# One written order for all engines over the attention, the first weights and the first nine steps

## The chip, the core and the metric

The kernel runs on one core of one Trainium2 chip. The metric is device time in microseconds (us), from three runs before the change. Engines are called by the profile's names: PE (TensorE, matmul), PEld (its weight load), DVE (VectorE), ACT (ScalarE), POOL (GpSimd) and SP (SyncE, which issues all DMAs here).

## The reference, cut to what matters

Attention between x (4 batches, 8 heads, 512 tokens, 64 wide) and a state of 32 rows per head, in both directions; then two dense feed-forward layers over the 2176 rows of 512 that come out. Weights come as float64, x and state as float32.

```python
a = softmax(scale * x @ state.T);  xread = a @ state         # 512 rows per batch and head
a2 = softmax(scale * state @ x.T); sread = a2 @ x            # 32 rows per batch and head
x = concat(xread, sread) -> (4 * 544, 512)
h = x @ moe_w_in                                             # 512 x 2048
x = (maximum(h, 0) + log1p(exp(-abs(h)))) @ moe_w_out        # softplus, 2048 x 512
g = x @ w_gate; val = x @ w_val                              # 512 x 1536 each
out = (g * sigmoid(g) * val) @ w_out2                        # 1536 x 512
```

## The kernel before, in words

**Precision.** Matrices are float32 split in two parts of a shorter format, a high part (a copy on ACT) and a low part (whole less high, on POOL or DVE, line 77); a product is three matmuls (`mm3`, line 74). A weight arrives as int64 raw words (`Piece`, line 101): 128 rows x 512 values, 512 KB. `head` is two DVE instructions on the upper words (lines 117, 121), `square` is ACT (line 127), `tail` is two on DVE (line 131 for the lower words, line 135, which multiplies by a comparison with TINY so that values too small become zero). Then `high` (ACT, line 141) and `low` (POOL). w_in is used whole (t of the piece), w_out split.

**Attention.** There are eight items (b, par), each four heads of one batch: 128 rows (4 heads x 32 state rows) by 512 tokens. Scores on PE (line 259), row maximum on DVE (264), its negation (266), exponent with row sum on ACT (269), transposition of the scores in blocks of 32 on DVE (273), maximum over groups of 32 (280), subtraction on POOL (283), exponent on ACT (288), sums (292 to 295) on DVE, product on POOL (298), transposition back on DVE (304), high and low part (308, 77) into aT. Besides, PE transposes the first exponent (322), ACT copies it (324), PE multiplies it with x (334), ACT scales it (338), and after two items PE turns the result (342, "psr") and ACT copies it into sw (343).

**First layer.** The first product, of attention weights by state by w_in, is taken as (state @ w_in) first: m, in `m_mm` (line 353), with high on ACT (357) and low on DVE. w_in and w_out are cut in four chunks of 512 columns. A unit is (chunk c, batch b, ft), 64 in all. `p1` is six matmuls (three per par) into a "ph" bank; ACT reads it twice for the softplus (high 383, whole 386), POOL makes the low part l (`g_low`, 77); `p2` is twelve matmuls into four banks "py" that collect over the four ft of a batch. After ft 3 `y_add` takes the four banks to yacc: DVE copies for chunk 0 (line 428), DVE additions after that (line 430). In step n, PE runs p2 of unit n and p1 of unit n + 4 (LAG). The rows of the state go through s1 to s4 once per chunk (s1: line 482).

**Order.** Hooks `at(n, kind, fn)` hang pieces of other work on the steps: in a step the kinds run as load, pe, softplus, dve0, y_add, act, g_low, pool, y_add, dve1, act1, pool1. `tc.manual_schedule(engines=...)` binds an engine to the order in which the program issues. For the attention that is PE alone, for the main loop PE, DVE and SP; ACT and POOL are ordered by the framework's scheduler by its own estimate. The attention is issued by `place(when, fn)` with times that sort it; all weights of the first chunk go through `whole` there, in the gaps.

**Loads.** All go by SP in order: the state, x transposed in halves of 64 partitions of 256 KB (`load_xt`, line 95: item par 0 the lower half of two tiles, par 1 the upper), x in rows (`load_xn`, 99) 512 KB per item, pieces. xT has four buffers, so that x of the last batches waits for the first scores.

**Second layer.** Lines 797 to 898; its weights are made in the background during the first layer (`second_piece`, EARLY: 18 of 36 pieces) and in its own steps. Per column block PE forms seven products px, pz, py ("quad"), ACT copies them (854, 866, 873), DVE adds (862, 877, 881, 886). Sums of y for it (T, lines 446 to 452, and their low parts) are made on DVE and POOL in the last steps of the first layer.

Of the kernel before, what the change touches and what calls it, by code (L numbers as in the profile page):

```python
# [16 lines left out]
P = 128  # L17

TINY = 1.125 * 2.0 ** -30
# [3 lines left out]
def attention_moe_moe2_kernel(  # L23
# [37 lines left out]
    SLOTS = {"aT": 8, "mt": 8,  "wo": 6, "yacc": 8, "s": 2, "xT": 4, "T": 14, "made": 3, "w2": 4, "gw": 8}  # L61
# [28 lines left out]
    def load_xt(b, par):  # L90
        q = slice(par * D, (par + 1) * D)
        for h in range(2):
            if par == 0:
                xT[b, h] = slot([P, 2, S], F32, "xT", f"xT{b}_{h}")
            nc.sync.dma_start(out=xT[b, h][q], in_=xt_d[b, h, q])
# [4 lines left out]

    class Piece:


        def __init__(self, views, tag, name):
            self.tag, self.name = tag, name
            self.raw = rawp.tile([P, 512], I64, tag="raw", name=f"raw_{name}")
# [5 lines left out]

        def head(self):

            self.t = rawp.tile([P, 512], F32, tag=f"t{self.tag}", bufs=6 if self.tag == "win" else 2, name=f"t_{self.name}")
# [12 lines left out]

        def tail(self):
            ti = self.t.bitcast(I32)  # L130
            nc.vector.scalar_tensor_tensor(
                out=ti, in0=self.bot, scalar=29, in1=ti, op0=ALU.logical_shift_right, op1=ALU.bitwise_or,
            )
# [12 lines left out]
        def whole(self):  # L146
            for step in (self.head, self.square, self.tail):
                step()
            if self.tag != "win":
                self.high()  # L150
                self.low()

# [783 lines left out]
```

## Time and profile before

| | |
|---|---|
| runs | 791.03, 794.01, 796.45 us; median 794.01 |
| profiled execution | 790.25 us, its span 788.5 us |
| mean granted clock of PE | 0.984 |
| busy PE, PEld, DVE | 742.0, 576.4, 493.9 us |
| busy ACT, POOL | 320.3, 397.2 us |
| DMA | 143.79 MB, mean 182 GB/s |

The span is from the first to the last instruction of the profiled execution. Busy times of matmuls are modelled at their ends, and matmuls overlap. A row with "idle before us <-" gives the time that the engine waited just before such instructions, and what ended the wait.

### The profile page before, as it was taken

The page shows a single profiled execution, that of the slowest core. Times are in us where ns is not written, and L with a number is a line of the kernel's source. Part 1 is how long each engine was busy: PE and PEld are TensorE (multiplying, and loading weights), DVE is VectorE, ACT ScalarE, POOL GpSimd, SP SyncE. Part 2 cuts the span into 40 slices and gives each one's busy share as a digit, 9 for nine tenths or more (in the row PEclk, how much of TensorE's full clock was granted, in tenths as well). Part 3 has the DMA queues.
Part 4 walks back from the last instruction along what each step waited for, and adds up shares of the span by engine and source line. Part 5 has one row for each costly group of instructions (what it writes and reads, how often), then busy time and mean ns, then how long its engine had stood idle before and what let it go on. Part 6 is the DMA issues. An engine that isn't in the chain of part 4 may idle for free.

```text
span 788.5 us, 10190 instructions
## 1 busy us (share of the span) xinstructions
PE 742.0 (94%) x3640; PEld 576.4 (73%) x3640; DVE 493.9 (63%) x697; ACT 320.3 (41%) x576; POOL 397.2 (50%) x352
## 2 busy tenths in 40 slices
PE   7476989999999999998789999999999999999997
PEld 2234756777777777786677888888888888888885
DVE  4899447766878668789657857675563343333343
ACT  3456433543444445454354444433253223323320
POOL 2367426444655555789468667665355113212311
PEclk9997998999999999999899999999999999999999
DMA  9942114343334333454939798978437646535502
GB/s 228 323 131 80 54 45 146 118 120 130 135 109 132 136 126 115 138 202 141 338 112 356 280 368 324 319 267 329 160 120 284 219 138 218 191 125 208 185 35 107
DMA packets 51202, 143.79 MB, mean 182 GB/s; under 512 B 5840, under 2 KB 18128, under 8 KB 51152
## 3 DMA queue, kind: packets, MB, share of 16 engines
q1 hardware_dynamic: 51152, 143.15, 53.6%
q8 instruction: 28, 0.46, 0.2%
q14 instruction: 22, 0.18, 0.1%
HBM read 107.22 MB, written 35.91 MB: 182 GB/s over the span
## 4 chain that ended last, share of the span: by engine, by line
PE 48%; DMA 1%; DVE 1%; ACT 1%; POOL 1%; issue 0%; ACTq 0%; DVEq 0%
PE po L74 16%; PE px L74 16%; PE pz L74 8%; PE py L74 6%; PE pt L74 3%; DMA gw<-gv_d 1%; DVE t_gv L121 0%; DMA gv_d<-gv 0%; POOL l L77 0%; DVE T L450 0%; PE pts L600 0%; POOL gv L77 0%; ACT h L551 0%; ACT cC L873 0%; DVE cA L881 0%
## 5 line engine op out<-in xcount | busy, mean ns | idle before, releaser
L74 PE MATMUL py<-h,wo 128*128 128x512 f32 x512 | 160.9, 396 | 10.7 <-DVE yacc L430 6.3
L77 POOL TENSOR_TENSOR l<-C,h 128x512 fp32r<-128x512 f32 x64 | 93.3, 1460 | 72.2 <-PE py L74 52.5
L74 PE MATMUL po<-w,h 128*128 128x512 f32 x384 | 126.3, 391 | 0.0
L74 PEld LDWEIGHTS py<-h,wo 128*128 128x128 f32 x512 | 97.1, 191 | 32.4 <-DVE yacc L430 7.1
L77 POOL TENSOR_TENSOR l<-cA,h 128x512 fp32r<-128x512 f32 x24 | 35.5, 1481 | 146.0 <-ACT h L551 146.0
L74 PE MATMUL ph<-aT,m 128*128 128x512 f32 x384 | 102.9, 406 | 0.0
L74 PE MATMUL py<-l,wo 128*128 128x512 f32 x256 | 101.1, 395 | 0.9 <-POOL l L77 0.9
L74 PEld LDWEIGHTS ph<-aT,m 128*128 128x128 f32 x384 | 72.5, 193 | 28.3 <-issue 11.5
L572 DVE TENSOR_TENSOR oacc<-po,oacc 128x512 f32<-128x512 f32 x80 | 54.7, 690 | 56.4 <-PE po L74 56.0
L74 PEld LDWEIGHTS po<-w,h 128*128 128x128 f32 x384 | 72.1, 188 | 14.8
L74 PE MATMUL po<-w,l 128*128 128x512 f32 x192 | 74.9, 390 | 0.5 <-POOL l L77 0.5
L74 PE MATMUL px<-T_0s,gw 128*128 128x512 f32 x216 | 61.0, 391 | 3.3 <-ACT cC L873 3.3
L74 PE MATMUL px<-T_1s,gw 128*128 128x512 f32 x216 | 60.7, 390 | 0.0
L74 PEld LDWEIGHTS py<-l,wo 128*128 128x128 f32 x256 | 48.8, 191 | 11.8 <-POOL l L77 1.4
L383 ACT ACTIVATE h<-ph 128x512 fp32r<-128x512 f32 x64 | 38.0, 593 | 33.8 <-PE ph L74 33.7
L74 PEld LDWEIGHTS px<-T_0s,gw 128*128 128x128 f32 x216 | 40.1, 188 | 12.7 <-ACT cC L873 4.1
L862 DVE TENSOR_TENSOR cA<-py,cA 128x512 f32<-128x512 f32 x24 | 16.5, 689 | 49.7 <-PE py L74 47.4
L74 PEld LDWEIGHTS px<-T_1s,gw 128*128 128x128 f32 x216 | 40.6, 188 | 8.5
L189 POOL TENSOR_TENSOR sums_gv<-t_gv 128x128 f32<-128x128 f32 x48 | 25.1, 541 | 40.4 <-DVE t_gv L135 40.4
L551 ACT ACTIVATE h<-cA 128x512 fp32r<-128x512 f32 x24 | 15.2, 632 | 71.7 <-DVE cA L881 70.4
L430 DVE TENSOR_TENSOR yacc<-py,yacc 128x512 f32<-128x512 f32 x48 | 31.7, 687 | 17.3 <-PE py L74 17.3
L74 PEld LDWEIGHTS po<-w,l 128*128 128x128 f32 x192 | 36.1, 188 | 8.3 <-POOL l L77 1.0
(150 smaller groups left out, 1410.1 us busy)
## 6 DMA issues: line engine op xcount, KB each, us to landing
gw<-gv_d SPq DMA_DIRECT2D x96, 512.0 KB, 6.6
gv_d<-gv SPq DMA_DIRECT2D x24, 512.0 KB, 3.3
gv_d<-split_gv SPq DMA_DIRECT2D x24, 512.0 KB, 3.4
w<-w_d SPq DMA_DIRECT2D x24, 512.0 KB, 9.3
raw_win<-in_moe_w_in_dram SPq DMA_DIRECT2D x16, 512.0 KB, 4.4
raw_wo<-in_moe_w_out_dram SPq DMA_DIRECT2D x16, 512.0 KB, 3.9
raw_gv<-in_moe_w_gate_dram SPq DMA_DIRECT2D x48, 128.0 KB, 3.0
raw_gv<-in_moe_w_val_dram SPq DMA_DIRECT2D x48, 128.0 KB, 2.8
```

The source lines that it names most:

```text
L74: nc.tensor.matmul(o, a[s], b[t], start=first and i == 0, stop=last and i == 2, **k)
L77: eng.tensor_tensor(out=o, in0=whole, in1=high.bitcast(F32), op=ALU.subtract)
L189: nc.gpsimd.tensor_tensor(out=o, in0=x, in1=y, op=op)
L383: nc.scalar.activation(self.h, self.ps, AF.Softplus)
L430: nc.vector.tensor_tensor(out=v, in0=yps[dt], in1=v, op=ALU.add)
L551: nc.scalar.activation(h, src, AF.Copy)
L572: nc.vector.tensor_tensor(out=v, in0=ps, in1=v, op=ALU.add)
L862: nc.vector.tensor_tensor(out=c["A"], in0=y, in1=c["A"], op=ALU.add)
```

## The change

1. `Piece`: `head` and `square` become `size` (ACT: the upper words as floats times 2^-112 into t, so that small values become zero there) and a `head` of one DVE instruction on t; `tail` has two DVE instructions (sign bit from the upper words, bits of the lower words). The multiplication of line 135 is gone. In DVE instructions a piece costs three instead of four; ACT's step now comes first instead of second.
2. `load_xt` loads a whole 128-partition tile (512 KB); an item needs both tiles of its batch. xT has eight buffers, raw words of the first chunk six of their own, later pieces two, and the other tiles of the attention have their own buffers (t 8, a2 6, e 4, t2 3).
3. All 25 first loads are issued in one list, LOADS, ahead of all else. The rest up to step 8 is one written list, ORDER: items' steps (`STEPS`), pieces of w_in and w_out of chunk 0 ("i", "o") and of w_in of chunk 1 ("j"), m ("mm", "mh", "ml"), p1 ("p"), softplus ("sp"), g_low ("gl"), p2 ("P"), y_add ("y" with a to d). Items 6 and 7 stand ahead of 5 and 4. The sums' additions and reciprocals (`parts`, `parts_1`) are made once for both items of a batch. All engines but the DMA queues follow it: PE, DVE, SP, ACT and POOL are bound to the order issued, in the main loop too.
4. The main loop starts at step 9 (FIRST). s1 to s4 of chunk 0 come at steps 9 to 15 (before 7 to 13), m of chunk 1 at 9, 12, 15, 19 (before 8, 11, 15, 19), w_out of chunk 1 at 9, 10, 12, 13, the three early second-layer pieces of chunk 0 at 11, 14, 15.
5. `y_add` of chunk 0 copies two of the four banks on ACT. Second-layer steps keep their places, with `size` and `head` where `head` and `square` were.

```diff
-TINY = 1.125 * 2.0 ** -30
+LOADS = "st x01 w0 x00 x11 x10 w1 w2 x31 x20 x30 x21 w3 n11 o0 o1 n10 n00 n01 n21 o3 n30 n31 n20 o2"
+ORDER = (
+    "iab0 ihd0 itl0 sc0 sc1 ts0 mx0 ts1 sc2 M0 M1 mi0 nm0 mx1 iab1 mx2 mi1 ex0 ts2 e0 ihd1 iab2 sc3 S0 ex1",
+    "itl1 pa0 a0 ihd2 S1 nm2 M2 e2 r0 mi2 pa2 mx3 nm1 ts3 a2 ti0 nm3 e1 M3 ti1 e3 tu0 sc6 rc0 ex2 rc2 pa3 mi3",
+    "tu1 iab3 pa1 ts6 ah1 sc7 ihd3 ex3 oab0 M6 al1 sc5 a3 mx7 a1 ts7 pr3 mi6 ah0 ts5 oab1 al0 M7 pr2 ex6 M5",
+    "sr3 mx5 mi7 sr2 nm7 mx6 pr0 e7 mi5 nm5 S3 e5 st1 nm6 pa7 S2 e6 pr1 itl3 sr0 so1 pa6 ex5 r2 itl2 sc4 sr1",
+    "a6 a7 st0 S6 ti3 mm1 oab3 ts4 so0 ex7 pa5 mx4 ti2 mh1 pr6 tu3 a5 ml1 pr7 ah3 nm4 tu2 e4 al3 M4 mm0 ah2",
+    "S5 mi4 pr5 S7 mh0 rc4 oab2 ml0 al2 pa4 sr5 r6 ex4 p0 rc6 a4 S4 ti7 sr7 r4 sr6 mm2 sp0 ohd0 pr4 ohd1 otl0",
+    "p1 mh2 gl0 tu7 sr4 st3 owh0 p2 ml2 ah7 otl1 so3 sp1 st2 p3 owl0 owh1 mm3 so2 owl1 sp2 P0 gl1 mh3 sp3 ml3",
+    "gl2 mm4 jab0 gl3 p4 mh4 ohd2 ml4 ti4 P1 sp4 otl2 gl4 tu4 owh2 mm6 ah4 owl2 jab1 p5 mh6 ohd3 P2 sp5 jhd0",
+    "otl3 gl5 ml6 owh3 mm7 owl3 p6 mh7 jtl0 P3 sp6 al7 ml7 jab2 gl6 mm5 ti5 ya3 yd3 yb3 yc3 p7 mh5 ti6 tu5",
+    "ml5 ah5 P4 al4 tu6 sp7 al5 ah6 al6 p8 gl7 P5 sp8 jhd2 gl8 jtl2 p9 jhd1 P6 sp9 jtl1 gl9 jab3 jhd3 p10",
+    "jtl3 P7 sp10 gl10 p11 ya7 yb7 yc7 yd7 P8 sp11 gl11 p12",
+)
+FIRST = 9
...
+        def size(self):
+            self.t = rawp.tile([P, 512], F32, tag=f"t{self.tag}", bufs=6 if self.tag == "win" else 3, name=f"t_{self.name}")
+            nc.scalar.activation(self.t, self.top.bitcast(F32), AF.Copy, scale=2.0 ** -112)
+
         def head(self):
             ti = self.t.bitcast(I32)
             nc.vector.tensor_scalar(
-                out=ti, in0=self.top, scalar1=3, scalar2=0x3FFFFFF8,
-                op0=ALU.logical_shift_left, op1=ALU.bitwise_and,
+                out=ti, in0=ti, scalar1=3, scalar2=0x7FFFFFF8, op0=ALU.logical_shift_left, op1=ALU.bitwise_and,
             )
+
+        def tail(self):
             nc.vector.scalar_tensor_tensor(
-                out=ti, in0=self.top, scalar=-0x40000000, in1=ti, op0=ALU.bitwise_and, op1=ALU.bitwise_or,
+                out=ti, in0=self.top, scalar=-0x80000000, in1=ti, op0=ALU.bitwise_and, op1=ALU.bitwise_or,
             )
-        def square(self):
-            self.mag = self.top.bitcast(F32)
-            nc.scalar.activation(self.mag, self.mag, AF.Square)
...
             nc.vector.scalar_tensor_tensor(
                 out=ti, in0=self.bot, scalar=29, in1=ti, op0=ALU.logical_shift_right, op1=ALU.bitwise_or,
             )
-            nc.vector.scalar_tensor_tensor(
-                out=self.t, in0=self.mag, scalar=TINY, in1=self.t, op0=ALU.is_gt, op1=ALU.mult,
-            )
...
+        if c == 0 and dt % 2:
+            nc.scalar.activation(v, yps[dt], AF.Copy)
+        elif c == 0:
             nc.vector.tensor_copy(v, yps[dt])
...
-    M_STEPS = (8, 11, 15, 19)
+    M_STEPS = (9, 12, 15, 19)
...
-        with tc.manual_schedule(engines={ENG.DVE, ENG.SP}):
-            for n in range(1 - LAG, NU):
+        with tc.manual_schedule(engines={ENG.DVE, ENG.SP, ENG.Activation, ENG.Pool}):
+            for key in LOADS.split():
+                first_load(key)
+            for names in ORDER:
+                do(names)
+            room[0] = "m"
+            for n in range(FIRST, NU):
```

## Rows read from the trace of the kernel before

**Rows 1.** The page's busy table, PE's entry (us, share, instructions).
```profile
PE 742.0 (94%) x3640; PEld 576.4 (73%) x3640; DVE 493.9 (63%) x697; ACT 320.3 (41%) x576; POOL 397.2 (50%) x352
```

**Rows 2.** Windows by stage: us, busy time of each engine, clock, DMA share, GB/s.
```profile
0.00:73.18 73.18, 46.91 (x413) 21.52 (x413) 57.72 (x118) 35.59 (x73) 33.81 (x33) 0.93 0.68 197
...
114.50:125.50 11.00, 7.08 (x31) 3.95 (x31) 9.53 (x13) 3.87 (x7) 6.23 (x7) 0.69 0.68 231
125.50:340.00 214.50, 214.50 (x1046) 162.85 (x1045) 158.66 (x205) 102.12 (x187) 121.52 (x110) 1.00 0.38 125
```

**Rows 3.** PE's waits from 74 us on: for whom; us in total, times, longest.
```profile
PE py L74 <- DVE yacc L430: 6.3, 2, 5.0
PE py L74 <- DVE yacc L428: 3.9, 1, 3.9
PE px L74 <- ACT cC L873: 3.3, 2, 2.5
PE py L74 <- POOL l L77: 0.9, 1, 0.9
```

**Rows 4.** Groups of PE's instructions up to 73.18 us: busy, mean ns; idle before.
```profile
L334 PE MATMUL pr<-xn,a 128*32 128x64 f32 x256 | 8.2, 303 | 0.0
...
L353 PE MATMUL pm<-t_win,st 64*32 64x512 f32 x32 | 3.6, 985 | 0.0
L342 PE MATMUL psr<-ident,sr 128*128 128x128 f32 x4 | 1.9, 468 | 12.7 <-DVE m L77 8.7 <-ACT sr L338 4.1
```

**Rows 5.** DVE in order of time: start, us, instruction, idle before.
```profile
8.36 0.69 DVE L264 TENSOR_REDUCE mx<-sc 128x1 f32<-128x512 f32 x1 [8.36 <-PE sc L259]
...
109.28 0.83 DVE L117 TENSOR_SCALAR t_win<-raw_win 128x512 int32<-128x512 int32 x1 [16.00 <-PE ps L482]
...
117.14 2.48 DVE L428 COPY yacc<-py 128x512 f32<-128x512 f32 x4
...
378.45 2.47 DVE L430 TENSOR_TENSOR yacc<-py,yacc 128x512 f32<-128x512 f32 x4
```

**Rows 6.** Groups of DVE's instructions up to 74 us: busy, mean ns; idle before.
```profile
L273 DVE STREAM_TRANSPOSE t<-sc 128x512 f32<-128x512 f32 x8 | 5.7, 706 | 2.1 <-ACT e L269 2.1
...
L117 DVE TENSOR_SCALAR t_win<-raw_win 128x512 int32<-128x512 int32 x6 | 5.1, 845 | 3.6 <-DMA raw_win<-in_moe_w_in_dram 3.6
L135 DVE SCALAR_TENSOR_TENSOR t_wo<-raw_wo,t_wo 128x512 f32<-128x512 f32 x4 | 4.0, 1007 | 0.1
...
L293 DVE TENSOR_SCALAR s<-s 128x16 f32<-128x16 f32 x8 | 3.4, 428 | 0.0
...
L266 DVE TENSOR_SCALAR nm<-mx 128x1 f32<-128x1 f32 x8 | 1.1, 143 | 0.0
```

**Rows 7.** Tile raw_win up to 80 us: ns min/median/max, first and last start.
```profile
L117 DVE TENSOR_SCALAR t_win<-raw_win x6: 417/766/1489, 22.0 to 73.5; 128x512 int32<-128x512 int32 x6
...
L135 DVE SCALAR_TENSOR_TENSOR t_win<-raw_win,t_win x5: 651/679/1592, 28.0 to 78.5; 128x512 f32<-128x512 f32 x5
```

**Rows 8.** PE in order of time: start, us, instruction, idle before.
```profile
5.28 5.50 PE L259 MATMUL sc<-xT,st 64*32 64x512 f32 x16 [5.28 <-DMA xT<-in_xt_dram]
...
65.80 7.54 PE L74 MATMUL ph<-aT,m 128*128 128x512 f32 x24
```

**Rows 9.** Windows of 10 us, columns as in rows 2.
```profile
10.00:20.00 10.00, 9.66 (x94) 4.23 (x92) 8.61 (x23) 5.24 (x13) 4.19 (x4) 1.00 1.03 273
20.00:30.00 10.00, 6.75 (x53) 2.32 (x53) 6.42 (x18) 3.76 (x10) 3.73 (x3) 1.00 1.03 344
...
360.00:370.00 10.00, 10.00 (x46) 8.27 (x45) 9.93 (x9) 5.44 (x10) 10.00 (x9) 1.00 0.40 159
...
380.00:390.00 10.00, 10.00 (x39) 8.08 (x39) 4.62 (x8) 1.43 (x3) 3.42 (x3) 0.81 1.01 363
```

**Rows 10.** Groups of DVE's instructions from 340 to 379 us, line 135.
```profile
L135 DVE SCALAR_TENSOR_TENSOR t_w<-raw_w,t_w 128x512 f32<-128x512 f32 x2 | 2.6, 1306 | 0.0
...
L135 DVE SCALAR_TENSOR_TENSOR t_gv<-raw_gv,t_gv 128x512 f32<-128x512 f32 x2 | 1.5, 728 | 0.2
```

More of the change, by code (lines that the diff above doesn't have):

```diff
@@ L144, in low @@
             low(nc.gpsimd, self.out[:, 1, :], self.t, self.out[:, 0, :])
[L146 to L151, printed above, removed]
     def piece_win(c, kt):
-        return Piece([w_in[kt * P:(kt + 1) * P, c * CH:(c + 1) * CH]], "win", f"win{c}_{kt}")
+        return Piece([w_in[kt * P:(kt + 1) * P, c * CH:(c + 1) * CH]], "win", f"win{c}_{kt}", "raw" if c else "raw0")
     def piece_wo(c, ft):
         r0 = (c * FT + ft) * P
-        return Piece([w_out[r0:r0 + P, :]], "wo", f"wo{c}_{ft}")
+        return Piece([w_out[r0:r0 + P, :]], "wo", f"wo{c}_{ft}", "raw" if c else "raw0")
     gv_d = {}
@@ new lines, in attention_moe_moe2_kernel, with do @@
+        STEPS = {
[3 rows of a table added]
+        }
+        PIECE = {"ab": "size", "hd": "head", "tl": "tail", "wh": "high", "wl": "low"}
+        BATCH = {"mm": m_mm, "mh": m_high, "ml": m_low}
+        def do(names):
+            for name in names.split():
+                key = name.rstrip("0123456789")
+                k = int(name[len(key):])
+                if key in STEPS:
+                    getattr(todo[k], STEPS[key])()
+                elif key[0] in "io" and key[1:] in PIECE:
+                    getattr((win if key[0] == "i" else wo)[0, k], PIECE[key[1:]])()
+                elif key == "mm":
+                    m_mm(0, *divmod(k, 2), "m")
+                elif key in BATCH:
+                    BATCH[key](0, *divmod(k, 2))
+                elif key == "st":
+                    st_turn(k)
+                elif key == "so":
+                    st_out(k)
+                elif key == "p":
+                    p1(units[k])
+                elif key == "sp":
+                    sp[units[k]].high()
+                    sp[units[k]].whole()
+                elif key == "gl":
+                    g_low(units[k])
+                elif key == "P":
+                    run(k, "load")
+                    p2(units[k])
+                elif key[0] == "y":
+                    y_add(*units[k][:2], "abcd".index(key[1]))
+                elif key == "jab":
+                    win[1, k].size()
+                elif key == "jhd":
+                    win[1, k].head()
+                elif key == "jtl":
+                    win[1, k].tail()
@@ L690, in at_weights @@
             for m, kind, step in (
-                (n, "dve0", "head"), (n, "act", "square"), (n + late, "dve1", "tail"),
+                (n - 1, "act1", "size"), (n, "dve0", "head"), (n + late, "dve1", "tail"),
                 (n + late + 1, "act", "high"), (n + late + 1, "pool", "low"),
             )[:3 if store is win else 5]:
-                at(m, kind, lambda step=step: getattr(store[key], step)())
+                if m == FIRST - 1 and n == FIRST:
+                    m, kind = FIRST, "load"
+                if m >= FIRST:
+                    at(m, kind, lambda step=step: getattr(store[key], step)())
         for c in range(NCK):
@@ L752, in attention_moe_moe2_kernel @@
             at(NU - 3 + n, "load", load_w2, n)
[L753 to L767 removed]
+        with tc.manual_schedule(engines={ENG.DVE, ENG.SP, ENG.Activation, ENG.Pool}):
[5 more added lines that the diff above has]
+            for n in range(FIRST, NU):
                 run(n, "load")
[L769 removed]
+                if True:
                     u = units[n]
@@ L778, in attention_moe_moe2_kernel @@
                     sp[nx].whole()
-                last = n >= 0 and u[2] == FT - 1
+                last = u[2] == FT - 1
                 run(n, "dve0")
@@ L816, in attention_moe_moe2_kernel @@
             for kind, names in (
-                ((n, f"conv{2 * half}"), ("head", "square")), ((n, f"conv{2 * half + 1}"), ("tail", "high", "low")),
+                ((n, f"conv{2 * half}"), ("size", "head")), ((n, f"conv{2 * half + 1}"), ("tail", "high", "low")),
                 ((n + half, f"conv{2 - 2 * half}"), ("sums",)), ((n + half, f"conv{3 - 2 * half}"), ("split_sums",)),
```

194 lines of the change are left out of this document (78 added, 116 removed), and 3 rows, old and new, of the table STEPS.

## The prediction, made before the change was run

> **What bounds the kernel now.** I read first the page's busy table: TensorE (PE) is busy 742.0 of 788.5 us [rows 1], so all idle time of PE together is 46.5 us, and nothing done to the other engines can be worth more than that plus what a low clock costs. Then the windows by stage [rows 2]. From 125.5 to 340 us PE is busy all of the time at clock 1.00, and the reader should see that no edit to VectorE (DVE), ScalarE (ACT) or GpSimd (POOL) can gain anything there. The idle time lies in four places: 26.3 us before the first second-layer matmul at 73.18 us (73.18 less 46.91 busy), 3.9 us around 115 us, 6.3 us between 340 and 395 us, 3.3 us shortly after [rows 3]. The list of PE's waits [rows 3] names who ends the later ones, and the groups of PE's instructions up to 73 us [rows 4] those of the start: there it is DVE (8.7 us in one piece before the last state transpose); at 115 us the DVE copy L428; between 340 and 395 us the DVE add L430; after that ACT's copy L873. In the first stage DVE is the engine to follow. It is busy 57.72 of 73.18 us [rows 2], and its first work could only begin at 8.36 [rows 5]: 57.7 of 64.8 us.
>
> The end of the program hangs on PE from 73 us on. So the change is worth: how much earlier the first second-layer group (P0 in the written order, at 73.18 before) starts, plus what becomes of the three later holes. The set of PE work ahead of P0 is the same in both kernels (eight attention items, m for items 0 to 3, p1 of units 0 to 3), and so is the set after it; the shift of s1 from step 7 to 9 and of the m pairs by a step moves PE work inside a stretch that is full.
>
> **Part 1: the start, up to P0.** The new order is limited by DVE up to the m low part "ml0", after which PE can run "p0". I count DVE's list up to ml0. Full-width passes: 8 row maxima, 8 score transposes, 8 group maxima, 7 sums, 4 back transposes, 2 m low parts, 37 in all. Such a pass is shown with some 0.70 us [rows 6], and the next starts about 0.07 us before its end, so 0.62 us each, 22.9 us. Four heads of one instruction at 0.42 (its fastest, [rows 7]) less 0.07: 1.4 us. Eight tail instructions (two per piece instead of four in head and tail) at 0.61: 4.9 us. The small ones (8 negations, 3 of rc and 2 of r, which are two instructions each and now come once per pair of items) are 18 of some 0.1 us net (a negation is 0.143 [rows 6] less the overlap, r a little more): 1.8 us. Sum 31.0 us. ACT's list up to there is 21 us and POOL's 18, so neither sets the end by its sum.
>
> Contention comes on top. L117, L121, L131, L135 and the small add L293 take longer than alone while POOL works: 0.845 mean against 0.417 at best, 1.007 against 0.651 for the same work, and 0.428 for an add of only 16 elements a partition [rows 6, 7]. Over those five lines (43 instructions before 74 us, of whose seven groups three stand) the surplus over the fastest of each is 10.4 us, 0.24 each. Of the 31 us, 14 instructions are of that kind: 3.4 us. The Trainium skill (SBUF — State Buffer, "Who interferes with whom") says that the pair of ports that the two engines share is held for a whole instruction and the loser blocks entirely. POOL is busy 33.81 of 73.18 us before [rows 2], and half of an instruction of some 1.3 us times that share gives 0.30, near the measured 0.24, so the trace agrees; but POOL's list is packed into about 34 us afterwards, a share near 0.6, which by that rule makes 0.4 each, 2.3 us more, and a median of 769.3. I keep the measured 0.24 for the sum, and the 2.3 us in the range.
>
> When DVE starts. Before, the first scores start at 5.28 [rows 8] after the state (0.26 MB) and two half loads of 0.26, 0.78 MB, and the first maximum follows at 8.36 [rows 5]: 3.1 us for the first item on PE. After, item 0 needs both x tiles whole, and w0 is queued between them: 0.26 + 3 x 0.52 = 1.83 MB. The 1.05 MB more at 344 GB/s (the stretch of whole loads, [rows 9]) take 3.1 us, at 273 GB/s 3.9. I take 3.3, so scores at 8.6 and the first transposition on DVE at 11.7; the 1.6 us of w0's head and tail are hidden ahead of it. DVE's clock thus runs from 10.1. The Trainium skill (DMA: Bandwidth & Descriptors, "Rules for kernel authors") says that transfers to two halves of the partitions use the same engines one after the other, and asks for one whole transfer. The DMA share here is 1.03 both with and without half loads in flight, which agrees as far as engine time goes. By it the whole load brings no bandwidth, only the later first item; the rows show 273 GB/s with half loads and 344 without [rows 9], which is where a gain would come from. I count none: all 25 loads (12.9 MB at 344 GB/s) are in by some 41 us, and n31, the last one that PE needs ahead of mm0, by 39.
>
> Waits. DVE's waits before 74 us, beyond the first, were 6.8 us, 3.6 of them for loads of w that had waited behind x and xn. In the new order w2 and w3 are the 8th and 13th load, in by some 15 and 23 us, before their heads come up; I keep the other 3.2 us. The lower end is 0 (a written order that fits), the upper the whole 6.8 plus some 4 for a handover here and there, since every group goes DVE, POOL, ACT, DVE. So p0 is at 10.1 + 31.0 + 3.4 + 3.2 = 47.7 us.
>
> From p0 to P0 PE has four p1 (7.54 us before [rows 8], mostly at the low clock, as the mean of 0.93 up to P0 [rows 2] says; it may be as low again), mm2 and mm3 (3.6 us for four, [rows 4], 1.8), the read of item 4 (8.2 / 8 = 1.0) and two state transposes at 0.48: 11.3 us. sp0 with its table load and gl0 lie beside that (p1 to p3 run meanwhile), and so do oab0 to owl0 (DVE's list through otl0 is 34.4 + 4.9 + 3.2 + 10.1 = 52.6). **P0 at 59.0 instead of 73.18: 14.2 us gained**, and the 0.9 us that P0 then waits for POOL's l [rows 3] go too, since gl0 has 5 us. Ends: 53 (no waits, p1 at the high clock) to 67 (more waits, more contention): 20 to 6 us.
>
> After P0 the others must keep up with 35 us of PE work up to P8: DVE's list has 19 us left, ACT's 18, POOL's 25. Two places are tight: P2 needs owl2, which stands on POOL behind gl4 and so behind p4 (1.5 us of slack), and p8 needs al5 behind ti5, ti6 and al4 (none). I charge 1.5 us, with 0 and 6 as ends.
>
> **Part 2: the hole at 115 us.** DVE's head of the last piece of w_in waited 16.00 us for s1 on PE [rows 5], and behind it stood the copies L428 (117.14), for which PE waited 3.9 us [rows 3]. The stretch has a mean clock of 0.69 [rows 2], which is 6.8 of 11 us at the lower of the two levels, where PE does half its work: up to 3.4 us lost after the pause, and I take 3.0. In the new order the heads of all four pieces stand ahead of s1, which comes later, so their buffers cannot be those that s1 reads; y's copies are split over DVE and ACT, behind p11 on PE. **6.9 us gained** (ends 3 and 6.9). The size step on ACT adds a wait of its own: "jab2" stands ahead of yd3 and yb3, "jab3" ahead of sp10, yb7 and yd7, each waiting for a raw buffer to come free and its load. If cover is gone, P4 or P8 waits for a load, some 4 us each; I take 0, as jtl0 is done some 8 us before jab2's turn.
>
> **Part 3: 340 to 395 us.** DVE has hardly a pause there (9.93 of 10 us busy from 360 to 370, [rows 9]), and the add at 378.45 [rows 5] ended PE's 5 us wait. Four of the dropped multiplications (L135: 2.6 + 1.5 = 4.1 us, [rows 10]) stand ahead of it from 340 us. Without them the add comes 4.1 us earlier, PE's pause is 0.9, and the slow clock behind it (39 matmuls from 380 to 390 us against 46 from 360 to 370, [rows 9], 1.5 us, and some 0.4 just before) does not occur; the earlier 1.3 us go too. That makes 7.3 us; POOL is as full there as DVE and its work stays, now in written order, as is ACT's. I take **5.5 us** (ends -5 and 8.7).
>
> **Part 4: after 395 us.** ACT's L873 is late behind a wait for POOL; one DVE pass less per piece helps a little: **1.0 us** (ends 0 and 3.3 [rows 3]).
>
> Sum: 14.2 + 0.9 - 1.5 + 6.9 + 5.5 + 1.0 = 27.0 us. The profiled execution took 790.25 us, 1.75 more than its span, so 763.3 by its own time. It lies 3.8 us below the median of the runs, 794.01; from that, **767 us**.
>
> **The rivals.** (a) The written order fits better than I charge: P0 at 53, no tight place, holes closed: 20 + 0.9 + 6.9 + 8.7 + 1.5 = 38 us, 756. For it: DVE's sum is 31 us only. Against: handovers through four engines. (b) Each handover in the start costs as it did before, or contention is as the port rule has it: P0 at 66 to 67, and 1.5 to 4 us more behind it: 17 us gained, 777. For it: the state transposes alone, which stand at the end of this chain, cost PE 12.7 us of waiting before [rows 4]. (c) The start is gained but not part 3, since POOL is busy 10.00 of 10 us from 360 to 370 [rows 9]: 767 + 5.5 + 1 = 773.5. (d) The change does not do what it says for DVE: the head now waits for ACT's size, so that DVE stops where before only ACT did; in the start that is eight pieces by some 1 us, 775. (e) Slower: ACT and POOL are now bound to the written order in 55 steps of the main loop, where a softplus stands behind hooks that wait for DVE, POOL or PE. PE's waits for l are 0.9 us in the whole loop now [rows 3]; if in-order waiting costs PE over 0.5 us in each of the 55 steps, 27 us are gone; at 0.7 us a step the time is 794 - 27 + 38 = 805. Against: the softplus has three steps, some 12 us, of lead.
>
> **How the numbers follow.** My sum 0.43, (a) 0.19, (b) 0.16, (c) and (d) together 0.13, (e) 0.05, something between (b) and no change 0.04. The range for 8 in 10 goes from 752 (below (a), with some of its spread) to 783 (above (b)). About 1%, 8 us, is what a measurement of this kernel can tell from no change: faster 0.89, same 0.06, slower 0.05.
>
> **What would show it.** Right: the first scores near 8.6 us, p0 near 48, P0 near 59; DVE three instructions per piece; no PE wait for L428's counterpart near 100 us and no slow clock there; a PE wait under 1.5 us in the stretch that was 370 to 380; PE full elsewhere. Wrong: P0 after 66 us; PE waiting for softplus or for l in the loop; a new pause at P4 or P8; the 5 us pause still there.

## The result and the profile after

The changed kernel takes 769.36 us (median of four runs, 768.64 to 770.80) against 795.13 (791.03 to 796.45) for the kernel before, measured beside it: ratio 0.969, interval 0.965 to 0.973. The prediction was 767. The total is right; its terms are not, as the table shows. Times are of the two profiled executions (790.25 and 768.64 us, spans 788.5 and 766.9).

| | before | after | gain predicted | gain measured |
|---|---|---|---|---|
| first scores | 5.28 | 9.51 (predicted 8.6) | | |
| first p1 (p0) | 65.80 | 45.60 (47.7) | | |
| first second-layer group, P0 | 73.18 | 54.64 (59.0) | 14.2 | 18.5 |
| P0 to the first px | 318.9 | 315.0 | 11.8 | 3.9 |
| first px to the end of the span | 396.4 | 397.3 | 1.0 | -0.9 |
| span | 788.5 | 766.9 | 27.0 | 21.6 |

(11.8 is 0.9 - 1.5 + 6.9 + 5.5; the first px, the second layer's first matmul, stood at 392.1 and stands at 369.6 us.) From its own profiled time of before the sum made 763.3, which is 5.3 too low; by the median it came to 767, 2.4 too low, since the profiled execution of before was among the quicker ones.

The page's busy table after, which answers to [rows 1]: VectorE lost 92 instructions and 55 us of work, PE 10 us.

```profile
PE 732.2 (95%) x3640; PEld 571.1 (74%) x3640; DVE 439.3 (57%) x605; ACT 318.9 (42%) x584; POOL 386.2 (50%) x352
```

The stages after, columns as in [rows 2]; the first line is the stretch to P0, then four windows of 10 us (before: [rows 9]), the stretch where the hole at 115 us was, and the end of the first layer.

```profile
0.00:54.64 54.64, 37.94 (x412) 18.34 (x412) 40.73 (x82) 31.92 (x69) 23.10 (x26) 0.75 0.76 294
0.00:10.00 10.00, 0.49 (x8) 0.26 (x16) 1.12 (x2) 1.94 (x2) 0.70 (x6) 1.00 0.83 289
10.00:20.00 10.00, 4.03 (x36) 0.65 (x20) 9.16 (x18) 3.79 (x8) 2.05 (x2) 0.85 1.03 413
20.00:30.00 10.00, 9.24 (x68) 3.87 (x72) 8.52 (x21) 7.85 (x17) 7.65 (x7) 0.50 1.03 410
30.00:40.00 10.00, 9.60 (x134) 4.79 (x126) 9.88 (x20) 6.38 (x17) 4.80 (x4) 0.50 1.02 407
114.50:125.50 11.00, 11.00 (x62) 8.06 (x62) 7.46 (x7) 6.72 (x13) 5.63 (x4) 1.00 0.15 49
...
350.00:360.00 10.00, 4.80 (x20) 3.64 (x19) 9.96 (x9) 2.34 (x5) 7.67 (x5) 0.92 0.64 217
```

PE before P0 has 412 instructions, as before (413), but 16.7 us of idle time instead of 26.3. The loads run at 410 GB/s where before they ran at 273 and 344. At 115 us PE is full at clock 1.00. From 350 to 360 it is less than half busy. The clock column up to P0, 0.75 here and 0.93 before [rows 2], can't be compared between the two traces (see the last section). Three events of PE in order of time, which answer to [rows 8]: the first scores, p0 and P0.

```profile
9.51 1.96 PE L267 MATMUL sc<-xT,st 64*32 64x512 f32 x16 [9.51 <-DMA xT<-in_xt_dram]
...
45.60 1.96 PE L89 MATMUL ph<-aT,m 128*128 128x512 f32 x6
...
54.64 0.73 PE L89 MATMUL py<-h,wo 128*128 128x512 f32 x2
```

PE's waits after (whole execution; those past P0 answer to [rows 3]):

```profile
PE sc L267 <- DMA xT<-in_xt_dram: 10.0, 2, 9.5
PE py L89 <- DVE yacc L453: 6.8, 2, 5.2
PE pa L335 <- ACT e L280: 6.7, 4, 3.3
PE px L89 <- ACT cA L883: 2.5, 2, 1.5
PE py L89 <- POOL wo L92: 1.9, 2, 1.2
PE px L89 <- ACT cC L902: 1.4, 2, 0.7
...
PE ph L89 <- POOL aT L92: 0.5, 1, 0.5
```

The DVE copy's wait (L428, 3.9) is gone. The DVE addition's wait (L430 before, L453 after) is there as before, 6.3 then and 6.8 now: part 3 did not happen. New are 2.4 us for POOL's wo and aT, in steps P2, P3 and p8; P2 and p8 are the places called tight.

Here is why part 3 did not happen. DVE and ACT in order of time in the changed kernel, around the pause that ends at 358.88 us:

```profile
323.79 0.55 DVE L136 TENSOR_SCALAR t_gv<-t_gv 128x512 int32<-128x512 int32 x1 [3.26 <-ACT t_gv L132]
...
340.28 0.59 DVE L136 TENSOR_SCALAR t_w<-t_w 128x512 int32<-128x512 int32 x1 [2.19 <-ACT t_w L132]
...
344.60 1.78 DVE L475 TENSOR_TENSOR T<-yacc,T 128x512 f32<-128x512 f32 x1
...
358.14 2.47 DVE L453 TENSOR_TENSOR yacc<-py,yacc 128x512 f32<-128x512 f32 x4
360.54 0.68 DVE L475 TENSOR_TENSOR T<-yacc,T 128x512 f32<-128x512 f32 x1
```

```profile
322.05 0.63 ACT L197 ACTIVATE split_gv<-sums_gv 128x512 fp32r<-128x512 f32 x1 [5.08 <-POOL sums_gv L193]
...
323.11 0.65 ACT L132 ACTIVATE t_gv<-raw_gv 128x512 f32<-128x512 f32 x1
...
338.54 0.63 ACT L152 ACTIVATE gv<-t_gv 128x512 fp32r<-128x512 f32 x1 [3.33 <-DMA gv_d<-gv]
...
339.60 0.65 ACT L132 ACTIVATE t_w<-raw_w 128x512 f32<-128x512 f32 x1
```

ACT, now bound to the written order, stands 5.08 us for POOL's sums and 3.33 us for a DMA; the size (L132), whose loads were issued 11 us and more earlier, is queued behind, and DVE's head (L136) waits 3.26 and 2.19 us for it. That uses up the 4.1 us of multiplications that went. It is what the trace suggests; the experiments below show that it is not the whole cause. A second thing is in the DVE rows: the same addition L475 takes 1.78 us at 344.6, beside POOL, and 0.68 at 360.5, where POOL stands idle. One of POOL's instructions of that stretch:

```profile
347.50 1.74 POOL L92 TENSOR_TENSOR B_0s<-yacc,B_0s 128x512 fp32r<-128x512 f32 x1
```

### The profile page after: what moved, and what is told of

Its sections match the earlier page's. It is cut to its first block, busy times and chain, and to the rows that moved or that the text cites. A ratio compares the mean times of both kernels' runs of the same rounds, so it can differ in the third digit from the quotient of the medians.

```text
span 766.9 us, 9998 instructions
## 1 busy us (share of the span) xinstructions
PE 732.2 (95%) x3640; PEld 571.1 (74%) x3640; DVE 439.3 (57%) x605; ACT 318.9 (42%) x584; POOL 386.2 (50%) x352
## 4 chain that ended last, share of the span: by engine, by line
PE 81%; DMA 5%; DVE 5%; POOL 4%; ACT 2%; issue 2%; SPq 0%; ACTq 0%; DVEq 0%; POOLq 0%
PE py L89 22%; PE px L89 16%; PE po L89 16%; PE ph L89 9%; PE pz L89 7%; PE pt L89 3%; PE pm L374 2%; DMA gw<-gv_d 2%; DMA raw_gv<-in_moe_w_val_dram 2%; PE ps L505 2%; POOL l L92 1%; PE ps L89 1%; PE sc L267 1%; DMA xT<-in_xt_dram 1%; PE pa L335 1%
## 5 line engine op out<-in xcount | busy, mean ns | idle before, releaser
L92 POOL TENSOR_TENSOR l<-C,h 128x512 fp32r<-128x512 f32 x64 | 91.7, 1435 | 108.2 <-PE py L89 64.3
L92 POOL TENSOR_TENSOR l<-cA,h 128x512 fp32r<-128x512 f32 x24 | 33.7, 1402 | 147.0 <-ACT h L574 147.0
L89 PEld LDWEIGHTS ph<-aT,m 128*128 128x128 f32 x384 | 70.2, 188 | 28.9 <-issue 12.0
L902 ACT ACTIVATE cC<-px 128x512 f32<-128x512 f32 x24 | 14.3, 597 | 64.2 <-PE px L89 60.8
L453 DVE TENSOR_TENSOR yacc<-py,yacc 128x512 f32<-128x512 f32 x48 | 31.5, 686 | 16.1 <-PE py L89 15.9
```

The lines of the kernel that those rows point to most:

```text
L89: nc.tensor.matmul(o, a[s], b[t], start=first and i == 0, stop=last and i == 2, **k)
L92: eng.tensor_tensor(out=o, in0=whole, in1=high.bitcast(F32), op=ALU.subtract)
L453: nc.vector.tensor_tensor(out=v, in0=yps[dt], in1=v, op=ALU.add)
L902: nc.scalar.activation(c["C"], x, AF.Copy)
```

## The experiments

The runs were made on several chips, and each ratio is to runs of the kernel before on the same chip. The kernel before scatters (788 to 801 us over all of them), the runs of the changed one and of its variants stay within 2 to 4 us of each other (5.3 in experiment 6). So differences under 5 us are read between kernels that ran on the same chip (1 to 4, 5 to 8, 9 to 11), or as intervals between events within a trace: P0; P0 to the first s1 (35.0 us before, 49.0 after; the orders differ there, so these two are not comparable); first s1 to the first px (283.9 and 266.0; s1 stands two steps later in the new order).

**1 and 2. What the DVE operations are worth.** The changed kernel with a fourth operation, and the kernel before with three.

```diff
+            nc.vector.scalar_tensor_tensor(
+                out=ti, in0=self.bot, scalar=29, in1=ti, op0=ALU.logical_shift_right, op1=ALU.bitwise_or,
+            )
```

> The changed kernel with a fourth DVE instruction per piece put back (the last one, an OR with the same bits, is done twice, so it changes no value). Theory A, DVE's list sets the start: four more instructions ahead of ml0 at 0.61 us and 0.24 of contention make p0 3.4 us later (49.0 instead of 45.6), P0 near 58, and the DVE add that ends PE's pause near 358 us comes 4 us later, so 774 to 778 us. Theory B, the written order and the loads set it and DVE has slack: p0 moves by under 1 us, and the time stays within 1.5 us of 769.4.

Measured: 783.54 us (781.98 to 785.60), ratio 0.991 (0.988 to 0.995), 5 us and more above what theory A had. s1 to px took 275.7 instead of 266.0. The loss is spread over several waits for DVE. Three lines of them stand here, of which the changed kernel has only the first (the addition, 6.8 there), with the window of the stretch that was full before and after:

```profile
PE py L89 <- DVE yacc L456: 7.1, 3, 3.9
PE pm L377 <- DVE t_win L149: 2.6, 1, 2.6
PE ptgs L502 <- DVE m L92: 1.7, 1, 1.7
```
```profile
130.00:320.00 190.00, 186.02 (x894) 141.29 (x893) 152.69 (x183) 87.52 (x163) 111.44 (x100) 0.99 0.40 133
```

In the start, P0 came at 55.57, only 0.9 later than in the profiled execution of the changed kernel. But there PE was at the lower clock (0.50) until 44.3 us, and here the clock rose at 33.8. Nearer to it is experiment 4, with the same order up to P0, on the same chip, and with the clock up at 33.2 us. Against it p0 is 3.3 us later, where theory A had 3.4, and P0 2.7 (55.57 against 52.84). The wait of 2.6 us for t_win above ends at 40.16 us, in the start, and behind it the clock is down again until 44.1. So the fourth operations are not free in the start. p0 here, and in experiment 4:

```profile
46.30 0.47 PE L89 MATMUL ph<-aT,m 128*128 128x512 f32 x1
```
```profile
43.00 0.50 PE L89 MATMUL ph<-aT,m 128*128 128x512 f32 x1
```

The second kernel: `size` is called within `head`, the rest is `head` and `tail` of the changed kernel in the order of before.

```diff
+            nc.scalar.activation(self.t, self.top.bitcast(F32), AF.Copy, scale=2.0 ** -112)
...
-            nc.vector.scalar_tensor_tensor(
-                out=self.t, in0=self.mag, scalar=TINY, in1=self.t, op0=ALU.is_gt, op1=ALU.mult,
-            )
```

> The kernel before with the three-instruction pieces alone; ACT's size stands directly ahead of the head, and order, loads and buffers are those of before. Theory A: eight pieces' instruction less ahead of 73 us, at 0.61 to 0.85 each, bring P0 from 73.2 to about 67; the hole at 115 us stays (3.9 us and the low clock); between 340 and 395 us the add L430 comes some 4 us earlier, since ACT is not bound to an order: 795 - 6 - 6 = 783 us. Theory B, that the order does it: P0 moves by under 2 us, 789 to 795 us.

Measured: 789.92 us (783.95 to 795.41), ratio 0.998 (0.994 to 1.002): no gain that can be told from none. Its waits (L423 is the copy of chunk 0, L428 before):

```profile
PE psr L337 <- ACT sr L333: 13.5, 3, 7.5
PE sc L254 <- DMA xT<-in_xt_dram: 12.2, 2, 6.4
PE py L74 <- ACT C L381: 4.2, 1, 4.2
PE py L74 <- DVE yacc L423: 2.6, 1, 2.6
```

The wait for the addition (L430) is gone, as part 3 had it, and PE waits 4.2 us for the softplus instead; P0 was later, at 76.59. So three operations alone gain nothing that shows, and the order with four loses over half of its gain: the order needs them, in the start (some 3 us) and more so in the loop (some 9).

**3. Whole loads of x.** The changed kernel with each tile loaded in two halves.

```diff
-        nc.sync.dma_start(out=xT[b, h], in_=xt_d[b, h])
+        for par in range(NPAR):
+            q = slice(par * D, (par + 1) * D)
+            nc.sync.dma_start(out=xT[b, h][q], in_=xt_d[b, h, q])
```

> The changed kernel with each whole x tile loaded as two halves of 64 partitions. If the whole load gives the rate (410 GB/s between 10 and 40 us against 273 to 344 before): the 4 MB of x at about 270 instead of 410 GB/s take 5 us longer in sum, 1.5 of it ahead of the first scores, and p0 comes 2 to 4 us later, 771 to 774 us. If halves cost the same (same engines, same bytes): under 0.7 us of difference.

Measured: 770.75 us (770.34 to 773.88), ratio 0.975 (0.971 to 0.978). Its first windows of 10 us:

```profile
0.00:10.00 10.00, 0.00 (x0) 0.00 (x0) 0.00 (x0) 1.28 (x1) 0.70 (x6) 1.00 0.77 189
10.00:20.00 10.00, 5.79 (x32) 0.82 (x32) 7.16 (x13) 1.87 (x4) 2.05 (x2) 1.00 1.03 247
20.00:30.00 10.00, 5.48 (x23) 3.07 (x24) 9.11 (x21) 5.55 (x13) 4.06 (x4) 1.00 1.03 244
30.00:40.00 10.00, 8.40 (x120) 4.24 (x118) 7.93 (x15) 7.41 (x18) 5.57 (x5) 1.00 1.03 408
```

189, 247 and 244 GB/s against 289, 413 and 410, at the same DMA share of 1.03: a half load occupies the engines for longer per byte. First scores at 11.7, P0 at 58.38, 3.7 later than in the changed kernel, whose clock rose at about the same time (44.3 us, here 43.0); the kernel of the next experiment, with the same start but for the halves and on the same chip, had P0 at 52.84 and took 766.73. The stretch from 10 to 30 us holds whole loads of weights too, so the rate of the half loads alone is not above these figures.

**4. The matmuls m of two items together.** For items 4 to 7 the changed order makes m singly.

```diff
-    "gl2 mm4 jab0 gl3 p4 mh4 ohd2 ml4 ti4 P1 sp4 otl2 gl4 tu4 owh2 mm6 ah4 owl2 jab1 p5 mh6 ohd3 P2 sp5 jhd0",
+    "gl2 mm4 mm5 jab0 gl3 p4 mh4 mh5 ohd2 ml4 ml5 ti4 P1 sp4 otl2 gl4 tu4 owh2 mm6 mm7 ah4 owl2 jab1 p5 mh6 mh7 ohd3 P2 sp5 jhd0",
```

(ml7 goes behind ml6 in the next line, and the second of a pair has a bank of its own).

> The changed kernel with m of items 4 and 5, and of 6 and 7, made back to back into two banks, as the main loop does it, instead of one by one. Theory: a single item takes PE 1.06 us, two back to back 1.09 in sum, since they use different halves of the rows, so the two pairs take 2.0 us less of a full PE: 767.4 us, if no new wait for a bank appears. Rival: the second bank taken from p1 costs what is saved, 769 to 770 us.

Measured: 766.73 us, ratio 0.970 (0.967 to 0.973). One m singly, in the changed kernel, and two together, in this one (again so at 61.13 us):

```profile
57.57 1.06 PE L374 MATMUL pm<-t_win,st 64*32 64x512 f32 x8
```
```profile
55.79 1.09 PE L374 MATMUL pm<-t_win,st 64*32 64x512 f32 x16
```

Two items use different halves of PE's rows, and issued back to back their matmuls run beside each other. PE so has 2.0 us less to do (four times 1.06 against two of 1.09). But P0 to s1 took as long as in the changed kernel; the window of that stretch in the changed kernel, and here:

```profile
54.64:103.60 48.96, 46.55 (x226) 32.75 (x222) 25.98 (x31) 21.46 (x41) 27.29 (x21) 1.00 0.17 54
```
```profile
52.84:101.80 48.96, 44.65 (x226) 32.66 (x222) 25.37 (x31) 21.78 (x42) 27.47 (x21) 1.00 0.14 44
```

1.9 us less busy, the same length: PE was not the limit there. Its waits for POOL's wo and aT grew from 2.4 to 4.2 us. The total lies near the 767.4 expected, but not by the way expected: P0 is 1.8 us earlier, with the clock, and the stretch behind px 1.4 shorter.

**5 and 6. The size on ACT.** The size is issued a step earlier (the first two pairs of lines); then, in another kernel, the loop is cut in two at step 44 and ACT left to the scheduler in the second part (the last two lines).

```diff
-                (n - 1, "act1", "size"), (n, "dve0", "head"), (n + late, "dve1", "tail"),
+                (n - 2, "act1", "size"), (n, "dve0", "head"), (n + late, "dve1", "tail"),
...
-                if m == FIRST - 1 and n == FIRST:
+                if m < FIRST <= n:
...
+        with tc.manual_schedule(engines={ENG.DVE, ENG.SP, ENG.Pool}):
+            for n in range(44, NU):
```

> The changed kernel with ACT's size of each piece of the main loop issued one step earlier (n - 2 in place of n - 1), everything else in place. Theory C: between 320 and 360 us DVE lost the time of the dropped instructions again (3.3 and 2.2 us) because its head waited for a size that stood on ACT behind a copy which waited for POOL or a store; with the size a step ahead these two waits go, the DVE add comes some 5 us earlier and PE's pause of 5.2 us near 358 us and its slow clock go: 762 to 764 us. Theory D: DVE and POOL are full there by contention and the add is not earlier: pause above 3.5 us, 768 to 770 us.

> The changed kernel with ACT left to the scheduler's own order from step 44 on (POOL, DVE and SP stay bound). Theory C: the same two waits of DVE go or shrink, pause under 2 us, 763 to 766 us. Theory D: 768 to 770 us. A third outcome: ACT's free order puts a softplus behind something late, as it did for 4.2 us in the run of the old order with short pieces, and PE waits for ACT instead of DVE: 767 to 771 us.

Measured: 763.45 us (762.22 to 763.90), ratio 0.963 (0.957 to 0.970), and 763.41 (763.04 to 768.34), ratio 0.966 (0.957 to 0.974). In the first, DVE's waits for the size from 315 to 360 us are gone, others stand in their place, and PE's long pause has not moved (the changed kernel: 5.2):

```profile
DVE T_0s L92 <- ACT T_0s L485: 2.4, 1, 2.4
DVE B_0s L92 <- ACT B_0s L485: 2.4, 1, 2.4
```
```profile
PE py L89 <- DVE yacc L453: 6.4, 2, 5.3
```

In the second the wait for the addition is gone and one for POOL has come:

```profile
348.70 0.68 PE L89 MATMUL py<-l,wo 128*128 128x512 f32 x1 [4.71 <-POOL l L92]
```

So the wait for the size was a way in which the pause came about, not its cause: three orders, three last links, 5 us each time. Both totals fell where theory C had them, but not by its mechanism, since the pause stayed. By their ratios they can't be told from the changed kernel's 0.969. In the first, P0 is 2.3 us earlier and P0 to s1 3.4 shorter (experiment 9), while s1 to px took 266.5 us as against 266.0.

**7. The hole at 115 us.** The kernel before with eight places for t of w_in instead of six.

```diff
-            self.t = rawp.tile([P, 512], F32, tag=f"t{self.tag}", bufs=6 if self.tag == "win" else 2, name=f"t_{self.name}")
+            self.t = rawp.tile([P, 512], F32, tag=f"t{self.tag}", bufs=8 if self.tag == "win" else 2, name=f"t_{self.name}")
```

> The kernel before with eight buffers instead of six for the converted pieces of w_in. Theory: the hole at 115 us hung on the head that waited 16 us for s1 to give its buffer back; with eight that wait and the hole go, without any written order: 6 to 7 us less than before, 785 to 789 us. Rival: the space for it is taken elsewhere or another wait holds DVE there: within 2 us of before.

Measured: 784.31 us (781.42 to 793.44), ratio 0.988 (0.983 to 0.992), some 7 us off. The window, which answers to the second line of [rows 2]:

```profile
114.50:125.50 11.00, 11.00 (x61) 8.17 (x60) 7.55 (x9) 5.24 (x11) 4.45 (x3) 1.00 0.15 48
```

The 16.00 us wait of [rows 5] is gone too. In the kernel before, the hole was a matter of buffers alone, and it could have been closed by one number. That the written order closes it because its four heads stand ahead of s1 is read off the order and was not tried apart.

**8. A clock kept up.** 34 idle transpositions on PE in the start of the changed kernel: 16 ahead of the first scores and, in the next line of ORDER, 8 and 10 around the first turn of the exponents.

```diff
-    "iab0 ihd0 itl0 sc0 sc1 ts0 mx0 ts1 sc2 M0 M1 mi0 nm0 mx1 iab1 mx2 mi1 ex0 ts2 e0 ihd1 iab2 sc3 S0 ex1",
+    "iab0 ihd0 itl0 wm16 sc0 sc1 ts0 mx0 ts1 sc2 M0 M1 mi0 nm0 mx1 iab1 mx2 mi1 ex0 ts2 e0 ihd1 iab2 sc3 S0 ex1",
...
+                    for _ in range(k % 100):
+                        nc.tensor.transpose(warm[0][:, :P], ident, ident)
```

> The changed kernel with idle transposes of the identity on PE before the first scores and around the first two turns of the exponents (34 of them, into a bank that is free then), where PE waits. They change no result. Theory E: from 24 us on PE is busy without a pause at the lower clock (4 transposes in 1.11 us, later 0.66) and sets p0 together with DVE; if the clock stays up, p0 comes 2 to 3 us earlier (DVE waited 2.6 us in sum), 766 to 767.5 us. Rival: DVE alone sets it, or the clock falls all the same: within 1 us of 769.4.

Measured: 766.58 us, ratio 0.968 (0.962 to 0.974), P0 at 51.79. The clock fell all the same at some 23 us: eight score matmuls took 1.06 us at 21.02, sixteen 3.64 at 25.01. Experiments 5 and 6, on the same chip, had P0 at 52.31 and 53.04 without them, so 0.5 to 1.3 us at most, and totals 3 us lower. The total lies in the range of theory E, but what the theory rests on, a clock that stays up, did not happen.

**9. Where the earlier size had gained.** That kernel had no waits for POOL from 52 to 98 us, and P0 to s1 took 45.6 us. The addresses in the built programs showed another difference: the framework places tiles in SBUF itself, and the first twelve high parts h had eight places in the kernel before, three in the changed one, five in that of experiment 5. With three, ACT's h of one step waits for the last reader of another, three steps back. Here h has five places and C three, by name, and no other line differs.

```diff
-            ps, work.tile([P, 512], F32, tag="C", name=f"C{n}"), work.tile([P, 512], F32R, tag="GH", name=f"h{n}")
+            ps, work.tile([P, 512], F32, tag=f"C{len(sp) % 3}", bufs=1, name=f"C{n}"),
+            work.tile([P, 512], F32R, tag=f"GH{len(sp) % 5}", bufs=1, name=f"h{n}")
```

> The changed kernel with five places in SBUF for the high halves h and three for C, by name; everything else, and the order on each engine, as in it. In the changed kernel the built program put all h of the first layer into three places and C into two, so that ScalarE's h of step n+3 waits for the last output matmul of step n (9 waits, 23.9 us, in the window 44 to 100 us); in the program of the run with the sizes two steps early they happened to have five and three, and there were no such waits. Theory P (places): the gain of that run at 52 to 98 us was the places, not the sizes; here the 9 waits go, with them TensorE's 1.9 us for POOL's wo and most of 0.5 for aT; p from the first output step to the first s1 falls from 49.0 to some 46 us, total 769.4 - 2.5 to 4 = 765 to 767. Rival S (the sizes): nothing moves, 769 to 770.5, and the waits of P2 and P3 stay.

Measured: 764.91 us (764.07 to 765.87), ratio 0.967 (0.966 to 0.969). ACT's longest entry among its waits from 44 to 100 us, in the changed kernel and in this one:

```profile
ACT h L404 <- PE py L89: 23.9, 9, 4.2
```
```profile
ACT h L404 <- PE ph L89: 12.9, 8, 3.0
```

The wait for the reader (py) has gone; what is left is the wait for the input (ph). The window from P0 to s1, 48.96 us in the changed kernel (above):

```profile
52.20:98.90 46.70, 46.13 (x226) 32.81 (x222) 27.02 (x31) 22.63 (x42) 28.62 (x22) 1.00 0.15 46
```

The same work in 2.3 us less, PE's idle time down from 2.4 to 0.6. By ratios, 0.967 against 0.969, the total can't be told apart from that of the changed kernel, which ran on a different chip; the 2.3 us rest on the two traces.

**10. The three edits together.**

> The three single edits that won, together: places for h and C by name, the state matmuls of items 4, 5 and 6, 7 back to back, sizes two steps early. If they are worth what they were singly and are independent: pairs 2.0 to 2.6, places with early sizes 5.9 over the changed kernel: 769.4 - 8 = 761.5 (760 to 763). If the gains were one and the same (a shift that the loop swallows): 763 to 764, as the sizes alone. The pause near 350 us stays at 4 to 5 us in both.

Measured: 765.23 us (763.40 to 766.29), no better than experiment 9 beside it. P0 to s1 took 46.9 us; with the 2 us of matmuls gone, PE waited 1.8 us for wo and 0.7 for aT again. The gains were the same one.

**11 and 12. Less to do before the second layer.** Seven pieces of the second layer are made early in the last chunk; here five. First in the kernel of experiment 9, then in the kernel before.

```diff
-        EARLY += [((NCK - 1) * UC + n, 0 if n % 4 else 2) for n in (0, 1, 2, 4, 5, 6, 8)]
+        EARLY += [((NCK - 1) * UC + n, 0 if n % 4 else 2) for n in (0, 1, 2, 4, 5)]
```

> Five places for h, three for C, and in the last chunk of the first layer five early pieces of the second instead of seven (those of steps 6 and 8 go to the second layer). Theory D (the pause before 360 us is VectorE's and POOL's load there: every operation that ScalarE or SP gave way with went over to the next engine): with two pieces less, the pause of 5.2 us is below 2 and the second layer's first matmul comes 3 us or more earlier than in the run with the places alone; in the second layer each of the two pieces is made behind the matmuls at no cost or gives back up to 3. Total 1 to 4 under that run. Rival O (it is the place of one wait in the order, not the load): the pause stays at 4 to 5 us and the total is within 1 of that run, or above it by what the second layer pays.

> The kernel before with five early pieces instead of seven in the last chunk of the first layer; its own order, its four operations a piece. Theory D (load of VectorE and POOL in that chunk): the pause of 4.95 us at 379 us and the 1.31 at 357 are gone or under 1 together, the first px comes 5 to 8 us earlier against the first s1 (283.9 us in the kernel before), the total falls by 5 to 8 (784 to 786 against 791). Then the pause never hung on the operations' number or on who orders ScalarE and POOL, and the change could not have taken it away. Rival Q (there the four operations and the planner's order set it): a pause of 3 us or more stays, and the total is within 3 of before.

Measured: 756.93 us (755.93 to 758.44), ratio 0.958 (0.956 to 0.959), 8.0 us under experiment 9, twice what theory D had at most; and 782.10 (779.58 to 784.28), ratio 0.989 (0.986 to 0.991), 8.0 under the kernel before, where it had 5 to 8. The window of the pause in experiment 9 and in 11, and PE's waits for the addition there:

```profile
340.00:360.00 20.00, 14.44 (x58) 11.20 (x57) 19.01 (x16) 11.05 (x22) 14.55 (x10) 0.91 0.70 223
```
```profile
340.00:360.00 20.00, 19.71 (x90) 15.99 (x89) 18.80 (x19) 7.08 (x13) 10.99 (x7) 1.00 0.64 245
```
```profile
PE py L89 <- DVE yacc L454: 6.2, 2, 5.3
```
```profile
PE py L89 <- DVE yacc L454: 0.3, 1, 0.3
```

First s1 to first px fell by 8.4 us in both pairs (266.2 to 257.8, 283.9 to 275.5), and the rest of the span did not grow by more than 1.0 (399.0 to 399.4, 396.4 to 397.4): the two pieces are hidden in the second layer. In the kernel before, the wait of 6.3 us for the addition (L430) is gone as well, while the copy's at 115 us stays (3.5). DVE's waits for the size are still there in experiment 11 (3.6 and 3.4 us) and cost nothing. So the pause hung on how much the helpers have to do before the second layer, in the kernel before as in the changed one, and not on the order. Which helper it was is not shown: from s1 to px the two pieces take 5.9 us off DVE, 7.6 off POOL and 2.8 off ACT, and their loads go with them. The windows are not quite of the same work, since px stands at 365.13 in experiment 9 and at 357.24 in 11. Experiment 11 is the fastest version.

## Why the prediction was right, and where it was not

**Part 1, right in kind, 4.3 us too small.** First scores 9.51 for 8.6, DVE's first transposition 11.50 for 11.7, p0 45.60 for 47.7, P0 54.64 for 59.0. The 2.1 us up to p0 are no single term: DVE started 0.2 earlier, its list from there through ml0 (11.50 to 46.07) was busy 32.0 us where 32.8 were counted, its waits were 2.6 for 3.2, and PE began p0 0.5 before ml0 was done. From p0 to P0 it took 9.0 us, not 11.3, since the clock had risen by then (p1 1.64 us from 49 us on). That DVE's list sets the end holds where the clock is up: in experiments 4, 5, 9 and 10 PE stands 0.85 to 0.92 us within p0 for DVE's m, and a fourth operation makes p0 3.3 later (experiment 1). In the profiled execution of the changed kernel PE took part as well: at 0.50 of its clock, and 9.2 and 9.6 of 10 us busy from 20 to 40 us, it brought m so late that DVE waited 0.82 and 0.49 us for it. The prediction had no term for that. The clock rose at 44.3 us there and between 31 and 34 us in experiments 4 to 6 and 8 to 11, where p0 came at 41.9 to 43.8 and P0 at 51.8 to 53.0: mostly ahead of the best end that the prediction gave, 53. Why it rose at different times with the same order is open.

"Which is where a gain would come from. I count none": there was one. Loads of x in halves make P0 3.7 us later (experiment 3). It explains none of the 4.3, since the sum had the loads in time and the first scores came 0.9 after the forecast. The 344 GB/s taken for whole loads was itself a mixed stretch: three half loads of x were issued in it.

**Behind P0.** The tight places cost 2.4 us for the 1.5 charged, at the places named, but by another mechanism: h had three places in SBUF instead of eight, so ACT's softplus waited for PE's p2, and POOL's l and wo came late (the 23.9 us of ACT's waits and the 2.3 us that came back in experiment 9). The m made singly put 2.0 us more on PE; "the set of PE work ahead of P0 is the same in both kernels [...], and so is the set after it" overlooked it, though pairing them alone won nothing.

**Part 2, right:** the hole of 6.9 us is gone; in the kernel before, taking its cause away alone gave some 7 us (experiment 7).

**Part 3, wrong:** of 5.5 us came next to nothing. By the table P0 to px gave 3.9, and 0.9 + 6.9 - 2.4 - 2.0 leave 0.5 for it. The step that failed is "Without them the add comes 4.1 us earlier, PE's pause is 0.9": the pause was 5.2. The multiplications went, and DVE spent the time waiting for ACT's size (3.26 + 2.19 us), and where that wait was taken away, for other copies, or PE for POOL. The bound of the stretch was the work of the helpers together (experiments 11 and 12), and a term that takes the operations of one of them off the last link is not the gain. Rival (c) said so, by POOL's 10.00 of 10 us [rows 9], and had a share of the 0.13.

**Part 4, wrong:** 1.0 us expected, 0.9 lost (397.3 us, among 395.9 to 399.4 in the variants); the wait for cC fell from 3.3 to 1.4, one for cA of 2.5 came.

So the total came out by luck: a start 4.3 us better than charged, the offset of 3.8 us between the profiled execution and the median, and the loss of part 3 cancelled.

## What to carry to other kernels

Where helpers are close to full for 20 us ahead of a barrier (here the first matmul of the second layer), count what they have to do in that stretch and move work out of it: orders only choose which of them is last (5 us each time, three orders), while two pieces of work fewer gave 8 us, before and after the rewrite. After any change of order, look at how many places a rotating tile got: a wait for a reader (h for py) in place of a wait for an input (h for ph) is its mark. Before an operation is said to cost nothing in a stretch, compare executions in which the clock stood alike: against one that stood lower the fourth operation looked like 0.9 us in the start, against one that stood alike 2.7. And a rewrite's parts should be tried alone: three operations instead of four were worth nothing that shows in the old order and 14 us in the new one, and a hole that the new order closed was one buffer count.

## What was not expected of the hardware

- With loads of 64 partitions in the queue 244 to 247 GB/s moved (experiment 3, 10 to 30 us, loads of weights among them), with loads of 128 alone 407 to 413, at a DMA share of 1.03 in both. The Trainium skill (DMA: Bandwidth & Descriptors, "Rules for kernel authors") asks for whole transfers because two halves use the same engines in turn; the runs agree with the advice and show more than a lost overlap, 1.7 times the rate. "By it the whole load brings no bandwidth" was the prediction's own inference, and the runs contradict it.
- A DVE pass of 128x512 on two inputs in SBUF took 0.68 us alone and 1.58 to 1.78 beside POOL from 344.6 to 358 us, and POOL's own passes took 1.71 to 1.75 there, 1.30 at 338 us. The mean surplus of 0.24 us that the prediction used for the start hides that: where both are full, such a pass costs up to 1.1 us more. Not every pass does: the four additions of py, which lies in PSUM, took 2.47 us at 335.62 beside a busy POOL and 2.47 at 358.14 without it. The Trainium skill (SBUF — State Buffer, "Who interferes with whom") has the port held for a whole instruction, and the trace of 344 to 358 us agrees.
- The column of the granted clock says nothing about the time ahead of the first clock record of a trace; the view shows 1.00 there. That record stands at 56.0 us in the trace of before and at 13.6 us in that of the changed kernel. So the windows of before from 10 to 30 us show 1.00 [rows 9], but four transpositions of the exponent took 1.11 us there, as long as in the changed kernel at 34.86 us, where the column shows 0.50; later they take 0.66:

```profile
34.86 1.12 PE L335 MATMUL pa<-ident,e 128*128 128x128 f32 x4
...
45.18 0.66 PE L335 MATMUL pa<-ident,e 128*128 128x128 f32 x4
```

Where there is no record, the duration of one and the same operation is the hint at which of the two levels (1.2 and 2.4 GHz) held. By it PE was at the lower one in the start of before too, and the 0.93 up to P0 [rows 2], from which the prediction took the clock of p1, is too high.
